# Shifting expert slots between stages of a fused attention and PEER kernel by its table of rates

## The chip, the cores and the metric

The kernel runs on one core of a Trainium2 chip, in one launch. The metric is the device time of that launch in microseconds (us). The core has a matrix engine (PE, TensorE), a vector engine (DVE), an activation engine (ACT), a general engine (POOL, GpSimd), a queue engine that issues most transfers (SP), and 16 DMA engines.

## The reference

One input x of 2048 tokens by 512 is layer-normalised, and two branches of it are added to x: attention with 32 heads of 16 over one shared key and value head, and PEER, a mixture of 4096 single-neuron experts. Per token and head PEER scores 64 + 64 sub-keys, keeps the two best of each, keeps the two best of the four sums, and adds two experts, weighted.

```
xn = _layernorm(x, axis=-1)
return x + _A_ref(xn, A_wq, A_wk, A_wv, A_wo) + _B_ref(xn, B_w_q, B_k1, B_k2, B_u, B_v)
# _A_ref: scores = q k^T / 4 for 32 heads, p = softmax, o = p v, o @ wo
# _B_ref: i1, i2 = two best sub-keys of 64 on each side; cand = t1 + t2 (2 x 2)
#         top_e = two best of the four; g = softmax of their scores
#         act = gelu(xn . u[top_e]);  out = sum g * act * v[top_e]
```

So a token has 64 experts (32 heads by 2), each a row of u (512) and a row of v (512).

## The kernel before, in words

Tokens lie in 16 tiles of 128 and in four phases of four tiles. All four phases need attention and sub-key scores. The experts are done in two ways. For phases 0 and 1 they are **sparse**: one slot is one expert choice of each of 128 tokens, 512 slots in all (2 phases, 8 chunks of heads, 4 tiles, 8 choices). For phases 2 and 3 they are **dense**: a matrix of gates over all 4096 experts is made from one-hot rows, and all experts are multiplied.

A slot goes through three steps, each a function of the kernel:

- `gather` (L1058): POOL issues an indirect DMA that fetches 128 rows of 1024 values, u and v of an expert side by side, 512 KB, into one of 12 buffers named g.
- `dot` (L1070): DVE multiplies the u half with xn and sums it (one custom instruction and one that reads the accumulator). After every fourth slot three small DVE instructions (L1079 to L1081), a Tanh on ACT (L1086) and one more on DVE (L1093) make the weights of four slots.
- `add` (L1105): DVE adds weight times the v half into the token tile's sum xa. Only then is the buffer free: `gather` of slot m waits for `add` of slot m - 12.

The order of every engine's instructions is written out by the program. After a prologue (norm, projections, first scores) the main loop has 256 steps, counted by d. In a step PE makes four score tiles of attention (`scores`, L379), ACT takes their Exp (L386, four per step), PE multiplies four tiles with the values (`pv`, L396), and between them stand other threads of work: the sub-key thread (`wp_make`: expert weights for the sub-key scores are made from w_q, L550 to L560; `item`: psc products L598, then max and index on DVE, L611 and L613), the one-hot rows of a dense phase (`onehot`, L859 to L862, and their products L892), and its dense products (L800, L938).

How many slots a step does is set by one number, `pos`, which grows each step by a rate that depends on the stage, `dense_on[0]`:

```
            if dense_on[0] == 1:
                pos += 2.6 if d < half * 3 // 4 else max(0.0, NSL - pos) / max(half - 3 - d, 1)
            else:
                pos += (2.5 if len(IDX) < NC * TPH else 2.3 if 0 <= d - since < 12 else 1.75, 0, 1.0, 1.5, 0.5)[dense_on[0]]

            todo = max(min(int(pos + 0.001), g_next[0]) - d_next[0], 0) if d else 0
```

Stage 0 is the sparse part of the loop (its first rate holds while the indices of phase 0, NC * TPH = 32 of them, aren't all chosen, which is where expert weights are made), 4 comes just ahead of a one-hot stage, 2 is the one-hot stage (there are two, one for each dense phase), 3 its end, 1 the dense products. `half` is 256. `g_next`, `d_next` and `a_next` count the slots gathered, dotted and added. So the dots of a step are capped by what has been gathered, and gathering goes on to `a_next` + 12 at most, at the end of a step. A step on DVE runs: max and index of the sub-key thread, its `todo` dots, then up to max(`todo`, 3) adds with the small instructions between them, then the gathers on POOL. In steps 22 and 23 no adds are made (`quiet`, set where a pair of attention units is finished). While `lent` is 2, two of the 12 buffers serve another tile.

Of the kernel before, what the change touches and what calls it, by code (L numbers as in the profile page):

```python
# [33 lines left out]
NC = 8  # L34
TPH = GT
# [20 lines left out]
def tile_kernel(ctx, tc, x, wq, wkv, wo, wqT, kT, uv, ub, vb, out):  # L56
# [450 lines left out]
    def experts_out(t):  # L507
        acc, last = ACC[t], t // GT == QB[3]
        assert last or t in DONE_A
        store(lambda: nc.sync.dma_start(d_part[t] if last else out[t * P:(t + 1) * P, :], acc))  # L510
        LIVE.discard(t)
# [106 lines left out]
    IDX, G = {}, {}  # L618
# [470 lines left out]
    def weigh(n):  # L1089
        if n not in WT and n < a_ready[0] // SB:  # L1090
            ga, th = GA.pop(n), TH.pop(n)
            w = small.tile([P, SB], F32, name="w", bufs=3)
            nc.vector.scalar_tensor_tensor(w, th, 1.0, ga, op0=OP.add, op1=OP.mult)  # L1093
            WT[n] = w
# [17 lines left out]
    def gathers(most):  # L1112
        while g_next[0] < NSL and g_next[0] < a_next[0] + NGB - lent[0] and most > 0:
            gather(g_next[0])
            g_next[0] += 1
            most -= 1

    def dots(to):
        while d_next[0] < min(to, NSL):
            dot(d_next[0])  # L1120
            d_next[0] += 1

    def adds(most):
        while a_next[0] < a_ready[0] and most > 0:
            add(a_next[0])
            a_next[0] += 1
            most -= 1

    def tanhs(to):
        while a_ready[0] + SB <= to:  # L1130
            tanh(a_ready[0] // SB)
            a_ready[0] += SB
# [7 lines left out]
    def run(fns):  # L1140
        todo = fns[:]
        fns.clear()
        for fn in todo:
            fn()
# [6 lines left out]
    def flush():  # L1151
        posts()
        for _ in range(2):
            for fns in (ON_ACT, LAST, LATER, BEHIND):
                run(fns)
            ON_ACT.extend(LATER_ACT)
            LATER_ACT.clear()
        run(ON_ACT)
        run(BEHIND)
# [36 lines left out]
    dense_on, quiet = [0], [0]  # L1196
# [3 lines left out]
    def run_scores(until=None, key=None):  # L1200
        while (until is not None and spent[0] < until) or (key is not None and key not in IDX):
            posts()
            try:
                cost = next(sgen)
            except StopIteration:
                spent[0] = 1e9
                posts()
                return
            if cost is None:

                if key is None:
                    return
                continue
            spent[0] += cost
# [70 lines left out]
    def score_steps(n):  # L1285
        for _ in range(n):
            spent[0] += next(sgen)
# [113 lines left out]
    with tc.manual_schedule(engines=ENGINES):  # L1401
        nc.vector.tensor_copy(PK["mm"][96:128], PK["mm"][:32])
        run(AFTER)
        score_steps(3)
        done0 = spent[0] - 5.4
        half = STEPS // 2
        pos, since = 0.0, half
        for d in range(half + 24):


            if dense_on[0] != 0:
                since = d
            if dense_on[0] == 1:
                pos += 2.6 if d < half * 3 // 4 else max(0.0, NSL - pos) / max(half - 3 - d, 1)
            else:
                pos += (2.5 if len(IDX) < NC * TPH else 2.3 if 0 <= d - since < 12 else 1.75, 0, 1.0, 1.5, 0.5)[dense_on[0]]

            todo = max(min(int(pos + 0.001), g_next[0]) - d_next[0], 0) if d else 0

            def mid():  # L1420
                post = POST[:]
                POST.clear()
                for act, _ in post:
                    act()
                tanhs(d_next[0])
                run(ON_ACT)
                ON_ACT.extend(LATER_ACT)
                LATER_ACT.clear()
                run(LAST)
                LAST.extend(LATER)  # L1430
                LATER.clear()
                rest = BEHIND[:]
                BEHIND.clear()

                dots(d_next[0] + todo - 1)
                if a_ready[0] > a_next[0]:
                    weigh(a_next[0] // SB)
                dots(d_next[0] + 1 if todo > 0 else 0)
                for _, fn in post:
                    fn()  # L1440
                sums = min(a_ready[0] - a_next[0], max(todo, 3) if d < half else 4)
                if dense_on[0] > 2:
                    sums = min(sums, 2)
                if quiet[0] > 0:
                    quiet[0] -= 1
                    sums = 0
                if dense_on[0] == 2:
                    run(CHAIN)

                def go():  # L1450
                    n = sums
                    while rest or CHAIN or n > 0:
                        if n > 0:
                            adds(1)
                            n -= 1
                        elif not rest:
                            run(CHAIN)
                        if CHAIN:
                            CHAIN.pop(0)()
                        if rest:  # L1460
                            rest.pop(0)()
                    gathers(4)

                    for _ in range(1 if d < half - 4 else NT):
                        if OUTS:
                            experts_out(OUTS.pop(0))

                if dense_on[0] == 2:
                    POST_FILL.append(go)
                else:  # L1470
                    go()

            aim = done0 + (FILL - done0) * (d + 1) / half if d < half else 1e6

            def fill():
                run_scores(until=min(aim, spent[0] + MOST))
                run(POST_FILL)

            att_steps(d, mid, fill)
        flush()  # L1480
        run(STORES)
        while a_next[0] < NSL:
            dots(NSL)
            run(CHAIN)
            tanhs(d_next[0])
            adds(SB)
            run(STORES)
            gathers(NGB)
        assert not OUTS
        run(STORES)  # L1490


def build(nc, tc, args):
    tile_kernel(tc, *args)
# [33 lines left out]
```

## Time and profile before

| | before |
|---|---|
| median of 3 runs | 1872.38 us (1865.34 to 1872.58) |
| the profiled execution | 1873.29 us |
| its span, first to last instruction | 1871.5 us |
| granted TensorE clock | 0.997 |
| DMA traffic | 489.72 MB, mean 262 GB/s |

The profiled execution is 1.79 us longer than its span. In the views below a row has the start and the length in us or the busy time and the number of instructions; L12 is line 12 of the kernel. A name such as g<-in_uv_dram,idx is tile written <- tiles read.

### The profile page before, as it was taken

The numbers are of one execution on the slowest core, as the hardware profiler recorded it, in microseconds if no ns is written. First come the engines' busy times: TensorE is split into PE (matmuls) and PEld (weight loads), VectorE is DVE, ScalarE is ACT, GpSimd is POOL, SyncE is SP. The second block draws the span as 40 slices with busy tenths as digits, with TensorE's granted clock in tenths as the row PEclk, the third lists the DMA queues.
The fourth block names the chain that finished last, engine by engine and source line by source line (L and its number), as shares of the span: only waits on it lengthen the run. The fifth ranks groups of instructions, "written<-read, shape, count | busy, mean of one in ns | idle before, by whom it ended". The sixth has DMA issues, their size and how long they took to land.

```text
span 1871.5 us, 34947 instructions
## 1 busy us (share of the span) xinstructions
PE 1809.2 (97%) x10989; PEld 954.7 (51%) x10989; DVE 1629.8 (87%) x6378; ACT 1287.6 (69%) x1745; POOL 690.4 (37%) x920
## 2 busy tenths in 40 slices
PE   7999998999999899999999999999998999999998
PEld 4644444555554345555555554555543455555553
DVE  6749988999898977999899897999979778999994
ACT  4357665555558987888777555556579877778874
POOL 1124533435442122444344453345522124444430
PEclk9999999999999999999999999999999999999999
DMA  9699896996764777988899996877636868998982
GB/s 322 216 301 399 302 324 211 368 328 234 241 197 131 250 236 226 279 266 287 268 296 320 337 316 227 281 239 249 236 97 220 255 192 285 286 304 281 282 278 100
DMA packets 243704, 489.72 MB, mean 262 GB/s; under 512 B 93748, under 2 KB 106420, under 8 KB 243516
## 3 DMA queue, kind: packets, MB, share of 16 engines
q0 software_dynamic: 73728, 268.47, 42.9%
q1 hardware_dynamic: 168572, 218.21, 35.9%
q8 instruction: 87, 1.43, 0.3%
q10 hardware_dynamic: 1216, 0.79, 0.1%
q14 instruction: 101, 0.83, 0.1%
HBM read 426.49 MB, written 55.61 MB: 258 GB/s over the span
## 4 chain that ended last, share of the span: by engine, by line
PE 73%; DVE 7%; DMA 6%; ACT 5%; issue 3%; SPq 0%; POOL 0%; ACTq 0%; DVEq 0%; POOLq 0%
PE pv L396 21%; PE psc L598 17%; PE sc L379 15%; PE pact L800 8%; PE pout L938 8%; ACT pt L386 3%; PE pwo L494 2%; DMA g<-in_uv_dram,idx 2%; DVE xa L1105 1%; DMA wk<-dw 1%; DVE g L1070 1%; DVE oh L859 1%; PE pw L550 1%; DMA rsb<-dinv 1%; DMA gy<-dg 1%
## 5 line engine op out<-in xcount | busy, mean ns | idle before, releaser
L386 ACT ACTIVATE pt<-sc 128x1024 f32<-128x1024 f32 x1024 | 994.7, 1028 | 439.6 <-PE sc L379 380.4
L1058 POOL DMA_INDIRECT g<-in_uv_dram,idx x512 | 553.5, 1081 | 944.5 <-DVE xa L1105 429.0
L396 PE MATMUL pv<-pt,vaug 128*32 128x512 f32 x4096 | 495.8, 602 | 0.0
L379 PE MATMUL sc<-qa,kaug 64*128 64x512 f32 x2048 | 389.8, 451 | 23.0 <-ACT pt L386 18.9
L598 PE MATMUL psc<-wk,xt 128*128 128x512 f32 x1536 | 389.9, 401 | 5.2 <-DVE wk L560 4.1
L1105 DVE SCALAR_TENSOR_TENSOR xa<-g,w,xa 128x512 f32<-128x512 f32 x512 | 372.3, 745 | 0.1
L1070 DVE CUSTOM_DVE_ANT_0 g<-g,xa 128x512 f32<-128x512 f32 x512 | 335.5, 682 | 18.5 <-DMA g<-in_uv_dram,idx 18.5
L598 PEld LDWEIGHTS psc<-wk,xt 128*128 128x128 f32 x1536 | 277.4, 188 | 110.1 <-issue 43.1
L379 PEld LDWEIGHTS sc<-qa,kaug 64*128 64x128 f32 x2048 | 157.5, 184 | 342.3 <-ACT pt L386 210.1
L396 PEld LDWEIGHTS pv<-pt,vaug 128*32 128x32 f32 x4096 | 107.2, 109 | 243.7 <-issue 243.7
L613 DVE FIND_INDEX8 i<-m,psc 128x8 uint32<-128x64 f32 x1024 | 206.6, 222 | 0.8 <-issue 0.8
L938 PE MATMUL pout<-wk,wd 128*128 128x512 f32 x768 | 195.3, 401 | 4.3 <-DVE gy L981 2.1
L800 PE MATMUL pact<-xt,wk 128*128 128x512 f32 x768 | 196.1, 400 | 0.0
L938 PEld LDWEIGHTS pout<-wk,wd 128*128 128x128 f32 x768 | 140.4, 187 | 52.5 <-issue 4.9
L800 PEld LDWEIGHTS pact<-xt,wk 128*128 128x128 f32 x768 | 139.3, 188 | 48.8 <-issue 18.6
L611 DVE MAX8 m<-psc 128x8 f32<-128x64 f32 x1024 | 146.3, 215 | 18.2 <-PE psc L598 15.3
L765 DVE TENSOR_TENSOR wk<-rw,wk 128x512 fp32r<-128x512 f32 x128 | 85.2, 684 | 9.5 <-ACT wk L764 9.5
L941 DVE TENSOR_TENSOR da<-da,pout 128x512 f32<-128x512 f32 x128 | 83.1, 681 | 5.3 <-PE pout L938 5.0
L859 DVE TENSOR_TENSOR oh<-oh 128x2048 f16<-128x2048 f16 x64 | 78.0, 1219 | 2.7 <-ACT oh L826 2.7
L764 ACT CAST wk<-rw 128x512 fp32r<-128x512 f32 x128 | 74.1, 634 | 0.0
L613 DVE MATCH_VALUE_LOAD i<-m,psc 128x8 f32 x1024 | 72.4, 71 | 0.5 <-DVE i L613 0.5
L1093 DVE SCALAR_TENSOR_TENSOR w<-gth,ga 128x4 f32<-128x4 f32 x128 | 20.2, 158 | 50.7 <-ACT gth L1086 47.5
(162 smaller groups left out, 1315.2 us busy)
## 6 DMA issues: line engine op xcount, KB each, us to landing
wk<-dw SPq DMA_DIRECT2D x96, 512.0 KB
wqt<-in_wqT_dram SPq DMA_DIRECT2D x32, 512.0 KB
dw<-wk SPq DMA_DIRECT2D x32, 512.0 KB
rw<-in_ub_dram SPq DMA_DIRECT2D x64, 256.0 KB
rw<-in_vb_dram SPq DMA_DIRECT2D x64, 256.0 KB
gy<-dg SPq DMA_DIRECT2D x64, 256.0 KB
dg<-gst SPq DMA_DIRECT2D x14, 928.0 KB
g<-in_uv_dram,idx POOLq DMA_INDIRECT x512
```

The lines of the kernel that those rows point to most:

```text
L379: nc.tensor.matmul(p[:, b, :], kaug[o:o + 64, kc * P:(kc + 1) * P], QA[u][o:o + 64, i, :], start=True, stop=True)
L386: nc.scalar.activation(PT[u, kc, i], p, AF.Exp, scale=SCALE)
L396: nc.tensor.matmul(PV[u][32 * j:32 * j + 32, :], vaug[:, kc, :], pt[:, b, :], start=kc == 0, stop=kc == 15)
L598: nc.tensor.matmul(p, XT[k][:, a, j * P:(j + 1) * P], WC[n_][k][:, bb, :], start=n == 0, stop=n == 11)
L611: nc.vector.max(m8[:, jb, s, :], p[:, s * E:(s + 1) * E])
L613: nc.vector.max_index(i8[:, jb, s, :], m8[:, jb, s, :], p[:, s * E:(s + 1) * E])
L800: nc.tensor.matmul(p, us[:, a, k * P:(k + 1) * P], XT[k][:, c, :], start=n == 0, stop=n == 11)
L859: nc.vector.tensor_tensor(out=oa, in0=num(P), in1=bc(0, tb, P), op=OP.is_equal)
L938: nc.tensor.matmul(p, wd[0][:, a, j * P:(j + 1) * P], vs[:, c, :], start=n == 0, stop=n == 5)
L1058: nc.gpsimd.indirect_dma_start(out=gt, out_offset=None, in_=uv, in_offset=bass.IndirectOffsetOnAxis(ap=IDX[ph, c, ti][:, s:s + 1], axis=0))
L1070: nc.vector.tensor_tensor_reduce(u, u, XN[TPH * ph + ti], scale=1.0, scalar=0.0, op0=OP.mult, op1=OP.add, accum_out=a[:, i:i + 1])
L1105: nc.vector.scalar_tensor_tensor(acc, v, w[:, i:i + 1], acc, op0=OP.mult, op1=OP.add)
```

## The change

Two rates in the table change. While phase 0's indices are being chosen, a step does 2.8 slots instead of 2.5. In the one-hot stage of the first dense phase (d below 128), it does 0.5 instead of 1.0; the one-hot stage of the second dense phase keeps 1.0.

```
-                pos += (2.5 if len(IDX) < NC * TPH else 2.3 if 0 <= d - since < 12 else 1.75, 0, 1.0, 1.5, 0.5)[dense_on[0]]
+                pos += (2.8 if len(IDX) < NC * TPH else 2.3 if 0 <= d - since < 12 else 1.75, 0, 0.5 if d < half // 2 else 1.0, 1.5, 0.5)[dense_on[0]]
```

The order of the instructions on PE is the same in both kernels; on DVE, ACT and POOL the slots' instructions stand at other places, and a few transfers on SP with them. No tile and no transfer is added or taken away. Following the counters through the loop, before has 80 slots dotted after step 31 and the change 89; after step 60 it is 130 and 140, and after step 80, near the end of the first one-hot stage, 150 and 151.

On DVE at step 28 and the start of step 29, before (ISA rows of L1070 are dots, L1105 are adds, L611 and L613 belong to the sub-key thread, the numbers are those of buffers). The dots are those of slots 70 and 71, the adds those of slots 62 to 64:

```order
L1070 ISA g_3852,act_3920<-g_3852,xa_159 128x512
L1070 ISA act_3920 128x1
L1070 ISA g_3931,act_3920<-g_3931,xa_161 128x512
L1070 ISA act_3920 128x1
L1105 SCALAR_TENSOR_TENSOR xa_163<-g_3636,w_3923,xa_163 128x512
L1079 SCALAR_TENSOR_TENSOR gq_4016<-act_3920 128x4
L1093 SCALAR_TENSOR_TENSOR w_4021<-gth_4012,ga_3919 128x4
L1105 SCALAR_TENSOR_TENSOR xa_165<-g_3638,w_3923,xa_165 128x512
L1080 SCALAR_TENSOR_TENSOR gy_4017<-gq_4016,act_3920 128x4
L1105 SCALAR_TENSOR_TENSOR xa_159<-g_3640,w_4021,xa_159 128x512
```

The same place with the change, step 27, where the dots are those of slots 74 to 76 and the adds those of slots 65 to 67:

```order
L1070 ISA g_3893,act_3879<-g_3893,xa_159 128x512
L1070 ISA act_3879 128x1
L1070 ISA g_3895,act_3879<-g_3895,xa_161 128x512
L1070 ISA act_3879 128x1
L1070 ISA g_3897,act_3968<-g_3897,xa_159 128x512
L1070 ISA act_3968 128x1
L1105 SCALAR_TENSOR_TENSOR xa_161<-g_3445,w_3887,xa_161 128x512
L1079 SCALAR_TENSOR_TENSOR gq_3965<-act_3879 128x4
L1105 SCALAR_TENSOR_TENSOR xa_159<-g_3447,w_3887,xa_159 128x512
L1080 SCALAR_TENSOR_TENSOR gy_3966<-gq_3965,act_3879 128x4
L1093 SCALAR_TENSOR_TENSOR w_3974<-gth_3961,ga_3878 128x4
L1105 SCALAR_TENSOR_TENSOR xa_161<-g_3449,w_3887,xa_161 128x512
```

Before, the next step's first dot (slot 72) uses a buffer that add 60 freed a step earlier, and only its third (slot 74) uses one that add 62, above, frees. With the change the next step's three dots (77, 78, 79) use the three buffers that the adds above (65, 66, 67) free.

On DVE in the first one-hot stage, before: the one-hot rows (L859, L861, L862) with the dots of slots 144 and 145 and the adds of slots 140 to 142 between them:

```order
L1070 ISA g_7813,act_8403<-g_7813,xa_163 128x512
L1070 ISA act_8403 128x1
L859 TENSOR_TENSOR oh_8415<-oh_7451,oh_7453 128x2048
L861 TENSOR_TENSOR oh_7537<-oh_7451,oh_7453 128x512
L862 TENSOR_TENSOR oh_7537<-oh_7537,oh_7453 128x512
L1105 SCALAR_TENSOR_TENSOR xa_159<-g_7326,w_8401,xa_159 128x512
L1105 SCALAR_TENSOR_TENSOR xa_161<-g_7328,w_8401,xa_161 128x512
L1105 SCALAR_TENSOR_TENSOR xa_159<-g_7809,w_8401,xa_159 128x512
L1070 ISA g_7893,act_8403<-g_7893,xa_165 128x512
L1070 ISA act_8403 128x1
```

The same stage with the change, from the dot of slot 146 on:

```order
L1070 ISA g_7103,act_7813<-g_7103,xa_163 128x512
L1070 ISA act_7813 128x1
L859 TENSOR_TENSOR oh_8112<-oh_7511,oh_7513 128x2048
L861 TENSOR_TENSOR oh_7596<-oh_7511,oh_7513 128x512
L862 TENSOR_TENSOR oh_7596<-oh_7596,oh_7513 128x512
L859 TENSOR_TENSOR oh_8135<-oh_7511,oh_7513 128x2048
L861 TENSOR_TENSOR oh_7596<-oh_7511,oh_7513 128x512
L862 TENSOR_TENSOR oh_7596<-oh_7596,oh_7513 128x512
L859 TENSOR_TENSOR oh_8189<-oh_7511,oh_7513 128x2048
L861 TENSOR_TENSOR oh_7596<-oh_7511,oh_7513 128x512
L862 TENSOR_TENSOR oh_7596<-oh_7596,oh_7513 128x512
```

There is now a dot in every second step of this stage instead of in every step, and its adds come half as often. From step 32 to step 60 both kernels do 1.75 slots per step, the change some ten slots further on.

## The prediction

> **What bounds the kernel now.** First the page: which engine is busy and which one the chain of waits runs over.
>
> ```profile
> PE 1809.2 (97%) x10989; PEld 954.7 (51%) x10989; DVE 1629.8 (87%) x6378; ACT 1287.6 (69%) x1745; POOL 690.4 (37%) x920
> PE 73%; DVE 7%; DMA 6%; ACT 5%; issue 3%; SPq 0%; POOL 0%; ACTq 0%; DVEq 0%; POOLq 0%
> ```
>
> PE is busy nearly throughout and carries most of the chain. Its work is not touched, so the time can only change where PE waits: 62.3 us in all (1871.5 - 1809.2). Where that is shows the view of busy time by stage. I cut it at starts of steps, found by counting the Exp instructions (L386), four per step: the first row is steps 0 to 23 (expert weights are made), the second steps 24 to 31 (their end, up to where phase 0's indices are complete), the third steps 32 to 64, the fourth steps 65 to 80 (first one-hot stage); the last is a piece of the second.
>
> ```profile
> core 0: us, PE busy (x) PEld busy (x) DVE busy (x) ACT busy (x) POOL busy (x), PEclk, DMA share, GB/s
> 102.30:287.40 185.10, 178.32 (x1008) 84.70 (x1008) 150.89 (x757) 122.11 (x166) 73.09 (x93) 1.00 0.91 320
> 287.40:349.70 62.30, 58.52 (x329) 28.92 (x327) 54.93 (x282) 36.92 (x50) 29.71 (x41) 0.97 0.82 291
> 349.70:580.60 230.90, 229.15 (x1314) 126.82 (x1316) 211.84 (x1356) 137.62 (x171) 106.76 (x207) 1.00 0.76 253
> 580.60:663.20 82.60, 72.28 (x864) 33.35 (x856) 81.04 (x158) 77.64 (x105) 12.97 (x11) 1.00 0.57 184
> 320.00:325.00 5.00, 5.00 (x26) 1.33 (x25) 5.00 (x26) 2.48 (x4) 1.49 (x2) 0.66 0.95 324
> ```
>
> In the third row PE is the bound: 33 steps in 230.9 us, 7.0 us each, PE busy 99%. In the fourth, DVE is busy 81.04 of 82.6 us and ACT 77.64, so DVE is the bound and ACT stands close behind it. The second row is odd: 7.79 us a step (62.3 / 8), with PE and DVE both idle at times. What holds it, the chain of waits in that stretch tells:
>
> ```profile
> 292.43 5.69 DMA g<-in_uv_dram,idx
> 298.14 0.69 DVE g L1070
> 298.84 0.66 DVE xa L1105
> ...
> 301.44 5.29 DMA g<-in_uv_dram,idx
> 306.76 0.69 DVE g L1070
> ...
> 309.64 5.61 DMA g<-in_uv_dram,idx
> 315.27 0.69 DVE g L1070
> ```
>
> This is a ring: an add frees a buffer, a gather of 512 KB fills it in 5.29 to 5.69 us, a dot reads it, and the adds that free the next buffers stand behind that dot on DVE. It arises as no adds are made in steps 22 and 23 while dots go on: the 12 buffers run out, and three slots remain between what is dotted and what is gathered. Before leaves the ring by itself, since at 2.5 slots every second step has two dots and three adds.
>
> **The change part by part.** The price of a slot on DVE comes from the groups view:
>
> ```profile
> L1105 DVE SCALAR_TENSOR_TENSOR xa<-g,w,xa 128x512 f32<-128x512 f32 x512 | 372.3, 745 | 0.1
> L1070 DVE CUSTOM_DVE_ANT_0 g<-g,xa 128x512 f32<-128x512 f32 x512 | 335.5, 682 | 18.5 <-DMA g<-in_uv_dram,idx 18.5
> L1070 DVE DVE_READ_ACCUMULATOR2_ANT act<- 128x1 f32 x512 | 41.6, 81 | 0.0
> L1093 DVE SCALAR_TENSOR_TENSOR w<-gth,ga 128x4 f32<-128x4 f32 x128 | 20.2, 158 | 50.7 <-ACT gth L1086 47.5 <-issue 3.0
> L1080 DVE SCALAR_TENSOR_TENSOR gy<-gq,act 128x4 f32<-128x4 f32 x128 | 20.2, 158 | 1.2
> L1079 DVE SCALAR_TENSOR_TENSOR gq<-act 128x4 f32<-128x4 f32 x128 | 20.2, 158 | 0.4
> L1081 DVE TENSOR_TENSOR ga<-act,gg 128x4 f32<-128x4 f32 x128 | 20.1, 157 | 0.0
> ```
>
> A slot costs 0.682 + 0.081 + 0.745 and a quarter of the four small ones (0.631 / 4 = 0.158): 1.67 us of DVE. The Tanh on ACT, one per four slots, and the gather on POOL (busy 48% at most in these rows) move along and bind nothing.
>
> *Steps 1 to 24.* 62 dots become 68 and 53 adds 59: 6 slots, 10.0 us more for DVE. DVE idles 34.2 us there (185.1 - 150.89), so on average it fits: 161 of 185 us. But PE already idles 6.8 us at this load, and a DVE with less room answers psc and wk later. Between 0 (all in idle time) and +10.0 (all on the path) I take **+2.0**, close to the end that the idle time supports.
>
> *Steps 25 to 32, the ring.* Here the change bites. Following the counters: in before, slots whose buffer was freed only in the step ahead are three in step 25, two in 26, two in 27, and one in 28 and 29. With 2.8 slots nearly every step asks for three dots, and adds are three as well, so the distance between dotted and gathered stays at three: all three dots of each of steps 25 to 31, and both of step 32, wait for gathers issued at the end of the step before. How long a turn of the ring is shows POOL in order of time (a gather's issue):
>
> ```profile
> 292.43 0.94 POOL L1058 DMA_INDIRECT g<-in_uv_dram,idx  x1 [0.31 <-DVE m L611]
> ...
> 301.44 0.94 POOL L1058 DMA_INDIRECT g<-in_uv_dram,idx  x1 [0.30 <-DVE m L611]
> 302.68 0.94 POOL L1058 DMA_INDIRECT g<-in_uv_dram,idx  x1 [0.31 <-issue]
> ...
> 309.64 1.20 POOL L1058 DMA_INDIRECT g<-in_uv_dram,idx  x1 [0.31 <-DVE xa L1105]
> ```
>
> The third gather of step 24 starts at 292.43 and its dot was waited for; the third of step 25 starts at 302.68. A turn with three fresh dots is 10.25 us. With two fresh dots it runs from second gather to second gather: 301.44 to 309.64, 8.20 us. So the change takes 7 turns of 10.25 and one of 8.20 from step 24 to step 32: 79.95 us. Before needs, from the first add of step 24 to that of step 32:
>
> ```profile
> 288.59 0.75 DVE L1105 SCALAR_TENSOR_TENSOR xa<-g,w,xa 128x512 f32<-128x512 f32 x1
> ...
> 355.83 0.75 DVE L1105 SCALAR_TENSOR_TENSOR xa<-g,w,xa 128x512 f32<-128x512 f32 x1
> ```
>
> 67.24 us, in which DVE has fallen 5 us further behind PE (1.2 us after the step's start at 287.4, 6.1 after that at 349.7); I allow the change the same lag and no more, since PE already waits for DVE's wk in this stretch. Difference: **+12.7 us**. Ends: if all turns were 8.20 us, 65.6 - 67.24 = -1.6. If a gather took as long as the slowest that the chain shows,
>
> ```profile
> 122.88 10.12 DMA g<-in_uv_dram,idx
> ```
>
> a turn would be 4.4 us longer, and eight of them +48; that was one gather, in a stage with a DMA share of 0.91 and right at the loop's start, while the ring's own three lie within 0.4 us of each other, at a share of 0.82. I stay with these. The Trainium skill (DMA: Bandwidth & Descriptors, Anatomy of one DMA) prices a GpSimd transfer at about 2.0 us plus its bytes over 436e3 per us, 3.2 us for 512 KB as an estimate; by it a turn would be about 7.8 us and this term would vanish. The rows above don't agree with it here: 5.29 to 5.69.
>
> *Steps 33 to 64.* The lead of ten slots stays, the rate is 1.75 in both: nothing.
>
> *Steps 65 to 80.* 16 dots and 16 adds become 8 and 8: 8 x 1.67 = 13.3 us less for DVE, 67.7 us busy. ACT's 77.64 us then bind, so of 82.6 us at most 5.0 can go; the least is 0. I take **-3.5**, nearer the upper end, as ACT's Exp still wait at times for score tiles that PE makes behind the one-hot products.
>
> *After step 81* the change is one slot ahead until it evens out: nothing.
>
> Sum against the profiled execution: 1873.29 + 2.0 + 12.7 - 3.5 = 1884.5, so **1884 us**. The median before is 0.9 us lower; the same shift from it gives 1883.6.
>
> **The rivals.**
>
> *The gathers keep up (not slower).* The ring's turn falls to what PE needs, because a slower ring also thins the traffic that its gathers share. It decides where a gather lands in about 2.3 us (10.25 - 7.0 = 3.25 less than 5.6) or where PE, which needs psc and wk from DVE, can run ahead through the stretch. Then steps 24 to 32 cost no more than before, or lose their old waits, and what is left is the one-hot gain: 1873.3 - 5.0 = 1868 to 1873.3 + 2.0 - 3.5 = 1872. For it: DVE has room on average, in every row. Against it: the three gathers of the ring took 5.69, 5.29 and 5.61 us and grew no faster as the ring slowed. By the skill's formula above this rival would win.
>
> *Stalls cool PE (slower still).* PE in order of time, before and behind the one long wait of this stretch:
>
> ```profile
> 310.46 1.92 PE L396 MATMUL pv<-pt,vaug 128*32 128x512 f32 x16
> ...
> 318.91 0.96 PE L598 MATMUL psc<-wk,xt 128*128 128x512 f32 x3 [2.72 <-DVE wk L560]
> ...
> 320.53 3.49 PE L396 MATMUL pv<-pt,vaug 128*32 128x512 f32 x16
> ```
>
> After 2.72 us idle the same 16 products take 3.49 us in place of 1.92, and the granted clock is 0.66 (row 320 to 325 above). If each of seven turns paid that 1.57 us on the path: 11.0 us more, 1895. I hold it for mostly hidden, since PE has 3.25 us to spare in a turn. The Trainium skill (TensorE: Matmul & The Clock Gate, Part 1) has the clock halve after an idle window of about 3.4 us; the trace agrees on the slowdown, here after a shorter wait. Gathers that land later in busier traffic lead to the same region.
>
> *DVE fills up ahead of the ring.* The 10 us of steps 1 to 24 land on the path: 1892.
>
> *The rate isn't followed.* The cap on gathers could undo the higher rate; but the counters show 89 slots for 80 after step 31, so the ring slows the steps and does not thin them: 1873.
>
> **How the numbers follow.** Forecast 0.55 (by its own terms 1878 to 1893: ring +10 to +15, steps 1 to 24 0 to +5, one-hot -5 to 0), gathers keep up 0.22, PE cools or gathers slow 0.15, DVE full 0.05, rate not followed 0.03. The range cuts about a tenth on either side: 1869 to 1900. A measurement of this kernel can tell about 0.5% from no change, 9.4 us: faster means below 1863.9, which only a full one-hot gain and a vanished ring could near: 0.03. Slower is above 1882.7: the upper two thirds of the forecast (0.37) and the two rivals above it (0.20), 0.57. The rest is the same, 0.40.
>
> **What would show it.** Right: the waits of DVE's dots for gathers grow from 5.4 us in this stretch,
>
> ```profile
> DVE g L1070 <- DMA g<-in_uv_dram,idx: 5.4, 5, 1.6
> ```
>
> to some 20 us (a turn of 10.25 less 6.9 us of DVE work, 54.93 / 8, seven times), nearly all between the ends of steps 24 and 32; these eight steps take 72 to 78 us in place of 62.3; the chain there shows seven or eight gathers; and the 16 one-hot steps take 78 to 80 us, with DVE below 70 us busy. Wrong: if the eight steps stay near 62 us, the ring is no bound and the first rival holds; if the one-hot steps don't get shorter, DVE was not what held them; if steps 1 to 23 grow by more than 5 us, DVE's room was an average only.

## The result, and the profile after

| | before | after |
|---|---|---|
| median | 1872.48 us (6 runs, 1865.34 to 1878.13) | 1893.81 us (6 runs, 1890.16 to 1902.01) |
| ratio to before | | 1.0129 [1.0108, 1.0151] |
| the profiled execution | 1873.29 us | 1902.01 us |
| its span | 1871.5 us | 1900.2 us |

The change makes the kernel 1.3% slower. The profiled execution of it was the slowest of its six; the experiments below ran the same kernel once more, and that profile (1892.69 us, span 1890.9) lies near the median. Both are used here and called the first and the second profile.

The page of the first: busy time per engine, and the shares of the chain of waits.

```profile
PE 1816.9 (96%) x10989; PEld 958.8 (50%) x10989; DVE 1629.4 (86%) x6378; ACT 1288.5 (68%) x1745; POOL 688.0 (36%) x920
PE 74%; DVE 9%; DMA 6%; ACT 3%; issue 1%; SPq 0%; DVEq 0%; ACTq 0%
```

DVE, ACT and POOL do what they did. PE's 10989 instructions are the same and take 7.7 us more, and PE's idle time has grown from 62.3 to 83.3 us (1900.2 - 1816.9). Where, shows the view of busy time by stage, cut at the same steps as before; here the first profile for steps 0 to 23, 24 to 31, 32 to 64 and 65 to 80, then 24 to 32 together.

```profile
core 0: us, PE busy (x) PEld busy (x) DVE busy (x) ACT busy (x) POOL busy (x), PEclk, DMA share, GB/s
101.70:292.50 190.80, 180.00 (x1008) 85.23 (x1008) 158.93 (x781) 122.59 (x167) 78.73 (x99) 0.99 0.92 326
292.50:364.20 71.70, 61.41 (x327) 29.91 (x325) 51.00 (x258) 36.86 (x50) 26.66 (x39) 0.93 0.74 248
364.20:608.10 243.90, 232.22 (x1314) 127.78 (x1318) 218.40 (x1390) 137.55 (x172) 112.45 (x211) 0.97 0.73 245
608.10:688.80 80.70, 71.37 (x864) 33.01 (x856) 74.32 (x133) 77.43 (x103) 7.89 (x6) 1.00 0.48 161
292.50:383.60 91.10, 69.83 (x368) 34.32 (x366) 61.97 (x332) 41.41 (x55) 30.58 (x42) 0.89 0.76 254
```

Steps 24 to 31 grew by 9.4 us (71.7 against 62.3), and the 33 steps behind them by 13.0. Nearly all of the latter is step 32: 383.6 - 364.2 = 19.4 us, against 6.8 before. PE, which had run ahead of DVE, waits for it there. So the region has to be cut behind step 32, and there before reads

```profile
287.40:356.50 69.10, 65.32 (x368) 32.67 (x366) 61.59 (x335) 41.40 (x56) 33.10 (x46) 0.98 0.84 295
```

69.1 us against 91.1. The view of waits of the first profile in these nine steps says who waits: engine, line, for what, us in total, times, longest.

```profile
DVE g L1070 <- DMA g<-in_uv_dram,idx: 28.1, 17, 5.7
PE psc L598 <- DVE i L613: 10.8, 1, 10.8
PE psc L598 <- DVE wk L560: 7.4, 2, 5.4
```

The dots wait 28.1 us for gathers, 17 times, and PE waits behind them, most of it once, at the end. The chain of waits of the second profile (start, us, what) gives seven gathers, one at the start of each of seven turns:

```profile
296.64 5.95 DMA g<-in_uv_dram,idx
...
307.14 5.24 DMA g<-in_uv_dram,idx
...
317.04 5.34 DMA g<-in_uv_dram,idx
...
326.86 7.43 DMA g<-in_uv_dram,idx
...
338.77 6.51 DMA g<-in_uv_dram,idx
...
349.85 6.58 DMA g<-in_uv_dram,idx
...
361.08 10.16 DMA g<-in_uv_dram,idx
```

A turn runs from one of these starts to the next: 10.50, 9.90, 9.82, 11.91, 11.08, 11.23, and the last runs to the gather at 375.73, shown further below, 14.65. The ring is there in every step from 24 to 31. Three turns are as long as forecast, four are longer, and their gathers landed later.

Lengths of stages in us, from the profiles of both kernels and of the experiments below (steps found as in the prediction):

| steps | before | after, 1st | after, 2nd | same_after_81 | no_ring | keep_three | middle_instead | rate_265 |
|---|---|---|---|---|---|---|---|---|
| 0 to 7 | 67.0 | 69.4 | 70.7 | 69.0 | 71.5 | 71.5 | 67.1 | 67.8 |
| 8 to 23 | 118.1 | 121.4 | 120.3 | 120.3 | 121.3 | 119.2 | 118.0 | 118.3 |
| 24 to 32 | 69.1 | 91.1 | 87.3 | 89.3 | 65.4 | 65.5 | 69.7 | 83.5 |
| 65 to 80 | 82.6 | 80.7 | 80.6 | 80.4 | 80.4 | 80.4 | 80.3 | 80.3 |

### The profile page after: what moved, and what is told of

Its sections match the earlier page's. It is cut to its first block, busy times and chain, and to the rows that moved or that the text cites. A ratio compares the mean times of both kernels' runs of the same rounds, so it can differ in the third digit from the quotient of the medians.

```text
span 1900.2 us, 34942 instructions
## 1 busy us (share of the span) xinstructions
PE 1816.9 (96%) x10989; PEld 958.8 (50%) x10989; DVE 1629.4 (86%) x6378; ACT 1288.5 (68%) x1745; POOL 688.0 (36%) x920
## 4 chain that ended last, share of the span: by engine, by line
PE 74%; DVE 9%; DMA 6%; ACT 3%; issue 1%; SPq 0%; DVEq 0%; ACTq 0%
PE pv L396 21%; PE psc L598 16%; PE sc L379 15%; PE pact L800 9%; PE pout L938 9%; DMA g<-in_uv_dram,idx 3%; PE pwo L494 2%; DVE xa L1105 2%; ACT pt L386 2%; DVE g L1070 1%; DMA gy<-dg 1%; DVE oh L859 1%; DMA rw<-in_vb_dram 1%; DVE m L611 1%; PE pw L550 1%
## 5 line engine op out<-in xcount | busy, mean ns | idle before, releaser
L1058 POOL DMA_INDIRECT g<-in_uv_dram,idx x512 | 551.4, 1077 | 977.7 <-DVE xa L1105 380.0
L1105 DVE SCALAR_TENSOR_TENSOR xa<-g,w,xa 128x512 f32<-128x512 f32 x512 | 374.2, 746 | 0.0
L1070 DVE CUSTOM_DVE_ANT_0 g<-g,xa 128x512 f32<-128x512 f32 x512 | 336.3, 684 | 44.1 <-DMA g<-in_uv_dram,idx 42.7
L613 DVE FIND_INDEX8 i<-m,psc 128x8 uint32<-128x64 f32 x1024 | 206.8, 224 | 0.0
L611 DVE MAX8 m<-psc 128x8 f32<-128x64 f32 x1024 | 146.5, 216 | 28.1 <-PE psc L598 27.5
L859 DVE TENSOR_TENSOR oh<-oh 128x2048 f16<-128x2048 f16 x64 | 78.0, 1219 | 4.1 <-ACT oh L826 2.6
L613 DVE MATCH_VALUE_LOAD i<-m,psc 128x8 f32 x1024 | 74.9, 73 | 0.0
L657 POOL CAST fi<-i 128x64 f32<-128x64 uint32 x32 | 8.9, 280 | 137.8 <-DVE i L613 137.6
```

The lines of the kernel that those rows point to most:

```text
L611: nc.vector.max(m8[:, jb, s, :], p[:, s * E:(s + 1) * E])
L613: nc.vector.max_index(i8[:, jb, s, :], m8[:, jb, s, :], p[:, s * E:(s + 1) * E])
L859: nc.vector.tensor_tensor(out=oa, in0=num(P), in1=bc(0, tb, P), op=OP.is_equal)
L1058: nc.gpsimd.indirect_dma_start(out=gt, out_offset=None, in_=uv, in_offset=bass.IndirectOffsetOnAxis(ap=IDX[ph, c, ti][:, s:s + 1], axis=0))
L1070: nc.vector.tensor_tensor_reduce(u, u, XN[TPH * ph + ti], scale=1.0, scalar=0.0, op0=OP.mult, op1=OP.add, accum_out=a[:, i:i + 1])
L1105: nc.vector.scalar_tensor_tensor(acc, v, w[:, i:i + 1], acc, op0=OP.mult, op1=OP.add)
```

## The experiments

**The change once more** gives a second profile. Here and below, the ratio is to the kernel before as it ran beside the kernel in question.

> The changed kernel itself once more, with a fresh profile. Its first profile was 28.7 us longer in span than before: 5.7 in steps 0 to 23, 22.0 in steps 24 to 32 (the ring of gathers), 7.9 in step 126 (one wait of DVE for the gates gy), and some 7 less in other places. Theory A (all three places are made by the order of instructions and come in every execution): 1890 to 1900 us, step 126 is again 12 us or longer. Theory B (step 126 was a single disturbed transfer): step 126 is about 6.9 us and the time nearer 1886.

Measured: 1895.27 us, ratio 1.0121 [1.0083, 1.0159]. In the first profile a single step far behind the change, step 126, had taken 14.7 us against 6.9 before: DVE waited 7.7 us for a load of dense gates.

```profile
996.92 11.80 DMA gy<-dg
```

In the second profile, with the order of instructions unchanged, the step is short again (last row of the stages of the second profile):

```profile
292.20:379.40 87.20, 69.04 (x368) 34.33 (x366) 61.91 (x332) 41.44 (x55) 30.23 (x42) 0.90 0.78 261
604.10:684.70 80.60, 71.29 (x864) 33.06 (x856) 74.28 (x133) 77.36 (x103) 7.90 (x6) 1.00 0.50 161
998.00:1005.60 7.60, 6.99 (x41) 3.75 (x39) 5.05 (x13) 5.95 (x10) 1.13 (x2) 1.00 1.03 348
```

So those 7.8 us belong to one execution and not to the change.

**Nothing moved behind step 81.** After step 80 the change is one slot ahead. A slightly lower one-hot rate takes that away.

```
-... 0.5 if d < half // 2 else 1.0 ...
+... 0.5 - 1.1 / 17 if d < half // 2 else 1.0 ...
```

> The change, but with a first one-hot rate of 0.5 - 1.1/17, so that from step 81 on the slots are the same as before (151 dotted, not 152) and SP's loads of phase 1's tiles stand again behind the loads of rw and gy. The ring is untouched. Theory A (one slot of lead moves those loads ahead of rw and gy on SP, which then wait for a store): step 126 is 6.9 us, about 8 us less than the changed kernel, 1884 to 1887. Theory B (disturbance, or DVE's load): no difference from the changed kernel, about 1893.

Measured: 1895.31 us, 1.0115 [1.0080, 1.0150], the same as the change beside it. What the change costs lies ahead of step 81. The next kernels build on this one where said.

**No pause in steps 22 and 23** (on same_after_81). The ring needs the pause, which runs the buffers down.

```
-                if d < 28:
+                if d < 20:
                     quiet[0] = 2
```

> As same_after_81, and adds go on in steps 22 and 23 (the pause after the pair of units at step 21 is left out), so that no dot of steps 25 to 33 needs a gather of the step just ahead; the same slots are dotted per step but for two. Theory A (the ring is the cost): steps 24 to 32 take about 9 x 7.0 = 63 us, less than before's 69.1; with 5 us for steps 0 to 23 and 3.5 gained in the one-hot stage 1866 to 1872. Rival (DVE is simply too full at 2.8 slots a step, and the ring only shows it): steps 24 to 32 stay above 75 us, 1880 or more.

Measured: 1870.98 us, 0.9983 [0.9967, 0.9999], and steps 24 to 32 in 65.5 us:

```profile
294.80:360.30 65.50, 63.80 (x368) 32.51 (x366) 61.40 (x339) 41.43 (x56) 30.75 (x44) 1.00 0.91 310
```

DVE is as busy as in the change (61.40 and 61.91 us) in 22 us less, and PE's clock is 1.00. So in these nine steps the rate of 2.8 and DVE's load are harmless, and the ring is the whole cost. Steps 0 to 23 still take 192.8 us against 185.1 before, so the higher rate isn't free there; in the total, the shorter steps 24 to 32 and the one-hot stage make up for most of it.

**Three gathered slots always in hand** (on same_after_81): another way out of the ring. The pause stays, but in steps 21 to 47 a step's dots stop three short of what has been gathered.

```
-            todo = max(min(int(pos + 0.001), g_next[0]) - d_next[0], 0) if d else 0
+            todo = max(min(int(pos + 0.001), g_next[0] - (3 if 20 < d < 48 else 0)) - d_next[0], 0) if d else 0
```

> As same_after_81 with the pause of adds in steps 22 and 23 kept, but in steps 21 to 47 dots stop three slots short of what has been gathered, so that none waits for a gather of the step just ahead; the slots held back are made up by step 48. Theory A: the ring is broken as in no_ring by another means, steps 24 to 32 take 63 to 68 us and the time is within 4 us of no_ring, 1867 to 1875. Rival (the pause itself is the cost, in that DVE loses two steps of adds and has to catch up): steps 24 to 32 stay above 75 us, 1880 or more.

Measured: 1865.24 us, 0.9961 [0.9943, 0.9979], which by the ratios is 1.5% or about 29 us under same_after_81, and the stage:

```profile
293.10:358.50 65.40, 63.70 (x368) 32.52 (x366) 61.33 (x335) 41.27 (x54) 33.52 (x45) 1.00 0.90 311
```

Two different edits that only break the ring give the same 65.4 to 65.5 us, and both are below before's 69.1: before, whose dots wait 5.4 us there, pays part of the ring too. The stage gives 23.9 of the 29 us (89.3 - 65.4); where the rest comes from was not taken apart.

**Half the step in the rate**, 2.65 where before has 2.5 and the change 2.8, with the one-hot rate set so that nothing moves behind step 81.

```
-... (2.5 if len(IDX) < NC * TPH else ... 1.0, 1.5, 0.5) ...
+... (2.65 if len(IDX) < NC * TPH else ... 1.0 - 4.80 / 17 if d < half // 2 else 1.0, 1.5, 0.5) ...
```

> Half the change: 2.65 slots a step early instead of 2.8, and the first one-hot rate lowered by just as many slots (4.8), so that from step 81 on all is as before. By the counters every step from 25 to 30 still asks for three slots gathered in the step ahead. Theory A (the ring sets the time): six turns of three fresh dots at 10.3 to 12 us and one of two, so steps 24 to 32 take 82 to 86 us, nearly all of the change's 87 to 91, and the time is 1886 to 1890. Rival (cost in proportion to the slots that are added early): half of the change's extra, 78 to 80 us there, 1882 or less.

Measured: 1881.59 us, 1.0055 [1.0036, 1.0074]; the stage:

```profile
288.60:372.10 83.50, 70.41 (x368) 34.61 (x366) 61.29 (x330) 41.51 (x55) 30.35 (x42) 0.90 0.79 265
```

Half the step in the rate costs 83.5 - 69.1 = 14.4 us in this stage, of the second profile's 18.1: four fifths of the cost for half of the slots, so it does not grow in proportion to them. The total is below the 1886 to 1890 us that were expected. Steps 0 to 23 cost only 0.9 us here; and the steps behind 126, in which the two kernels do the same, took 880.5 us in this profile against 886.0 before, which no edit explains.

**Before without the pause**: is there something to be won in before?

```
-                if d < 28:
+                if d < 20:
                     quiet[0] = 2
```

> The kernel before with the pause of adds in steps 22 and 23 left out, nothing else. Before has the ring too, for four steps. Theory A: steps 24 to 32 go from 69.1 to 64 to 66 us, 1868 to 1871. Rival (the pause keeps the reciprocal of the softmax sums and its transfers on time, and without it they cost what the ring saves): no change, 1872 to 1876.

Measured: 1870.85 us, 1.0002 [0.9983, 1.0021]. The dots' waits for gathers are gone, but steps 23 and 24 take 10.1 and 11.4 us in place of 8.4 and 8.0. The view of waits, 280 to 360 us:

```profile
DVE w L1093 <- ACT gth L1086: 4.8, 2, 3.0
...
PE pwt L557 <- DVE i L613: 2.5, 1, 2.5
```

DVE now waits for a Tanh of ACT ahead of an add, the adds that the pause held back stand ahead of its answers to PE, and PE waits for these. That this makes up the whole loss is a reading of the order, not shown by a run: in no_ring, also without the pause, the same two steps take 9.3 and 8.0 us. What is shown is that in before, leaving the pause out saves about as much as it costs. Keeping slots in hand leaves the pause and avoids the ring.

**The slots moved elsewhere**: early rate as before, the nine slots into steps 33 to 60.

```
-... 2.3 if 0 <= d - since < 12 else 1.75, 0, 1.0, 1.5, 0.5) ...
+... 2.3 if 0 <= d - since < 12 else 1.75 + 8.5 / 29 if d < 61 else 1.75, 0, 0.5 if d < half // 2 else 1.0, 1.5, 0.5) ...
```

> The one-hot half of the change alone, with the early rate left at 2.5: 0.5 slots a step in the first one-hot stage, and the 8.5 slots moved to steps 32 to 60 (1.75 + 8.5/29 a step), where there is no ring. From step 81 on as before. Theory A: steps 65 to 80 get 2 to 5 us shorter, nothing else moves, 1867 to 1870. Rival (steps 32 to 60 have no room: DVE 92% busy there becomes 98%): they get longer by 3 us or more and the time is 1872 or above.

Measured: 1870.6 us, 0.9974 [0.9956, 0.9992]. The steps that take the slots don't get longer (223.9 us for steps 33 to 64, 224.1 before), and the one-hot steps give 2.3 us (82.6 to 80.3).

**What makes the last landings late.** The view of SP in order of time (a row joins issues of one line) of the second profile, in the stretch of the late landings, and behind it POOL's last gather of the ring:

```profile
326.01 3.58 SPq L566 DMA_DIRECT2D dw<-wk  x2
329.69 4.01 SPq L572 DMA_DIRECT2D wk<-dw  x2
337.84 4.42 SPq L566 DMA_DIRECT2D dw<-wk  x2
342.35 1.50 SPq L572 DMA_DIRECT2D wk<-dw  x2
343.95 17.34 SPq L1172 DMA_DIRECT2D xt<-dxt  x16
361.34 2.66 SPq L572 DMA_DIRECT2D wk<-dw  x4
...
375.73 0.94 POOL L1058 DMA_INDIRECT g<-in_uv_dram,idx  x1 [0.31 <-DVE i L613]
```

From 326 us on SP issues stores of expert weights, reads of them and the next phase's token tiles; the seven gathers' late four start at 326.86 and after. How much all queues moved while a gather landed shows the view of busy time, its last number in GB/s; three of the seven:

```profile
317.04:322.38 5.34, 4.00 (x25) 2.80 (x21) 2.89 (x20) 3.23 (x6) 0.94 (x1) 1.00 0.71 241
349.85:356.43 6.58, 6.58 (x41) 3.52 (x39) 2.27 (x13) 3.88 (x4) 0.94 (x1) 1.00 1.06 355
361.08:371.24 10.16, 6.05 (x36) 3.07 (x34) 3.00 (x20) 2.75 (x4) 0.94 (x1) 1.00 0.98 342
```

That is 1.3, 2.3 and 3.5 MB (length times GB/s), and the three gathers of a step are 1.6 MB: in these three the landing grows with what is moved beside it. Two kernels on same_after_81 take transfers away. The first leaves the xt loads out:

```
-        if more and nph != ph:
+        if more and nph != ph and n_ != NC - 1:
             load_xt(nph, j)
```

> As same_after_81, but the 16 transfers of phase 1's transposed rows (xt<-dxt, 2 MB, issued by SP in the ring's last turns) are left out, so phase 1's scores come from phase 0's rows. The ring's last turn took 14.7 to 15.9 us, its gather landed in 10.2 to 11.4. Theory A (the gathers of the last turns land late as they share the DMA queues with SP's transfers): the last turn falls to 10.3 to 12 us, steps 24 to 32 to 84 to 86 us. Rival (the last turn is long for what PE and DVE do in it): it stays at 14 us or more, and steps 24 to 32 near 88.

Measured: 1891.11 us in one run, steps 24 to 32 in 86.1 us. The landing ahead of the last, which had stood beside the xt loads, is short now, and its turn is 9.86 us in place of 11.23; the last is still late:

```profile
351.49 5.20 DMA g<-in_uv_dram,idx
361.35 10.30 DMA g<-in_uv_dram,idx
```

SP's next four reads had moved up to stand beside it. The row joins them, issued from 358.40 on, with two that were issued at 343.52 and 344.00:

```profile
343.52 17.32 SPq L572 DMA_DIRECT2D wk<-dw  x6
```

The second leaves out four of SP's reads as well (chunk n = NC uses the tiles that are there):

```
         for k in ks:
+            if n == NC:
+                WC.setdefault(n, []).append(WC[n - 1][k])
+                continue
             wk = wk_tile()
```

> As no_xt_load, and the four reads of stored weights (wk<-dw, 2 MB) for the next chunk, which there simply took the place of the xt loads, are left out too: that chunk's scores use the chunk before's weights. In the ring's last three turns SP then moves nothing large. Theory A (gathers land late where SP's transfers share the queues): the third gathers of steps 29 to 31 land in 5 to 6 us in place of 6.5 to 10.3, these turns take 10 to 10.7 us, steps 24 to 32 81 to 84 us. Rival (the last turns are long for another reason): a landing of 10 us again in the last turn, 86 us or more.

Measured: 1885.44 us in one run, the stage in 82.6 us, and in the chain

```profile
326.65 7.26 DMA g<-in_uv_dram,idx
...
338.40 6.78 DMA g<-in_uv_dram,idx
...
349.74 6.32 DMA g<-in_uv_dram,idx
...
360.71 5.23 DMA g<-in_uv_dram,idx
```

The last landing falls from 10.30 to 5.23 us, and POOL's next third gather starts at 370.42 (three lines were added to this kernel, so its L1061 is L1058 of the others):

```profile
370.42 0.94 POOL L1061 DMA_INDIRECT g<-in_uv_dram,idx  x1 [0.31 <-DVE i L616]
```

That turn is 9.71 us (370.42 - 360.71) in place of 14.65. So SP's reads beside the gather made it late. The three turns before it stayed at 11.8, 11.3 and 11.0 us with landings of 7.26 to 6.32: SP's stores at 326 to 342 us were still there, and the four reads that are left stood at 342 to 345, behind the stores. With no_xt_load, the cause is shown for the last two of the four late landings. For the first two no kernel took the stores and reads beside them away; the traffic fits (in the second profile 2.5 and 2.4 MB were moved while they landed), but there it is not shown.

**A slow start** (on same_after_81): 2.5 slots in steps 0 to 3, then a little more than 2.8. In the second profile the third dot of step 2 had waited for a gather that was issued at the loop's start:

```profile
131.60 0.69 DVE L1070 CUSTOM_DVE_ANT_0 g<-g,xa 128x512 f32<-128x512 f32 x1 [8.76 <-DMA g<-in_uv_dram,idx]
```

```
-... (2.8 if len(IDX) < NC * TPH else ...
+... (2.5 if d < 4 else 2.8 + 1.2 / 28 if len(IDX) < NC * TPH else ...
```

> As same_after_81, but the first four steps keep the rate of 2.5 and the rest has 2.84, so that the lead at step 32 is the same. Theory A on steps 0 to 23 (the third dot of step 2 needs a gather that is issued only at the loop's start and lands behind SP's loads; that wait, and the clock after it, is half of the loss there): steps 0 to 7 go from 69 to 71.5 back to 67 to 67.5 us, steps 8 to 23 stay 1 to 3 us longer than before, the ring is as long as before this edit. Rival (DVE's load over all 24 steps makes it): steps 0 to 7 stay at 69 or above.

Measured: 1892.78 us in one run. Steps 0 to 7 take 66.6 us in place of 69.0 to 70.7, as expected; steps 8 to 15 take 61.8, 3.0 more than the kernel it was built on, so nothing was won.

**Put together**, for a kernel better than both. The first is middle_instead with three slots in hand (the two edits above); the second also spreads the slots of the second one-hot stage over the steps ahead of it.

> A version meant to beat both: middle_instead (2.5 early, the one-hot stage's 8.5 slots moved to steps 32 to 60) with dots that stop three slots short of the gathers in steps 21 to 47. Theory A: steps 0 to 23 as before (185), steps 24 to 32 65 to 66 us (before 69.1), the one-hot stage 2 us shorter: 6 us less than before, 1864 to 1868 where before is 1871 to 1874. Rival (what the ring no longer costs is lost elsewhere, as in before_no_pause): no different from middle_instead, ratio 0.997 to 1.000.

Measured: 1861.65 us, 0.9952 [0.9937, 0.9966].

```
-... 1.75 + 8.5 / 29 if d < 61 else 1.75, 0, 0.5 if d < half // 2 else 1.0, 1.5, 0.5) ...
+... 1.75 + 8.5 / 29 if d < 61 else 1.75 + 8.5 / 34, 0, 0.5, 1.5, 0.5) ...
```

> As middle_keep_three, and the second one-hot stage has the rate 0.5 too, its 8.5 slots moved to the steps from 146 to 179. Theory A: that stage (steps 184 to 199, 85.3 us before) gets 2 us shorter as the first did: 1862 to 1866 where before is 1871 to 1874. Rival (the steps from 146 on, or the dense stage after it, have no room for them): no gain over middle_keep_three.

Measured: 1858.52 us, 0.9940 [0.9916, 0.9963], the fastest of all. Its steps 24 to 32, and its first one-hot stage:

```profile
287.40:352.60 65.20, 63.72 (x368) 32.50 (x366) 61.27 (x337) 41.41 (x55) 33.22 (x45) 1.00 0.89 307
575.20:654.90 79.70, 71.51 (x864) 32.87 (x856) 73.18 (x131) 77.21 (x103) 7.76 (x6) 1.00 0.50 166
```

Its lead over middle_keep_three is inside the two intervals. What the second one-hot stage gave is not resolved: it took 82.3 us against 84.0, and it varies from 81.8 to 86.7 among kernels that do not touch it.

## Why the prediction was right or wrong

The direction and the mechanism held: the slots were bought in the one stage where a ring of gather, dot and add sets the pace, and no_ring and keep_three show that the loss in that stage is the ring's. The size did not: 1884 forecast, 1893.81 measured, about twice the loss. The time lies inside the range of 1869 to 1900. Three terms came out higher than forecast, and the total would be 4 to 5 us further off but for the last row below, places where the change does no other work. That is luck: no run explains it, and the steps behind 126 alone took from 880.5 to 888.9 us among kernels that do the same there. Term by term, as differences of spans of the profiles:

| term | forecast | 1st profile | 2nd profile |
|---|---|---|---|
| steps 0 to 23 | +2.0 | +5.7 | +5.9 |
| steps 24 to 32, the ring | +12.7 | +22.0 | +18.1 |
| steps 33 to 64 | 0 | +0.4 | +0.6 |
| steps 65 to 80 | -3.5 | -1.9 | -2.0 |
| step 126 | 0 | +7.8 | +0.7 |
| the rest | 0 | -5.3 | -3.9 |
| span | +11.2 | +28.7 | +19.4 |

*The ring*, forecast at +12.7 us and measured at +22.0 and +18.1, is the term that failed most, at the sentence "I stay with these": three landings of 5.29 to 5.69 us were taken for all turns, and the last four took 6.51 to 10.16. The turn of 10.25 us was right where it was measured: the first three turns of the second profile sum to 30.22 us against 30.75. The last four sum to 48.87 against 41.0, 7.9 more; their landings sum to 30.68 us against four times the mean of the three sampled ones, 22.1, which is 8.6 more. So the excess of the turns is the landings'. (All seven turns are 7.3 us over the forecast, more than the 5.4 by which the stage missed it; the 2 us between them were not taken apart.) The three sampled gathers landed between 298 and 315 us, and the trace of before had, in SP's order of time, what comes behind them:

```profile
318.88 3.58 SPq L566 DMA_DIRECT2D dw<-wk  x2
322.56 3.36 SPq L572 DMA_DIRECT2D wk<-dw  x2
...
333.72 21.18 SPq L1172 DMA_DIRECT2D xt<-dxt  x16
```

I took the price of a turn from the quiet half of the stretch and laid it over the busy half. The busy half had its price in the trace of before as well: taking the packets of POOL's queue in order, 144 to a gather, the last packet of the third gather of a step came 5.0 to 5.2 us after its issue up to 315 us, and 6.8 to 10.7 us after it from 318 to 356. The bound was there (a gather of 10.12 us), and was dismissed as one of another stage; the last landing came to 10.16 and 11.41. The formula of the Trainium skill (DMA: Bandwidth & Descriptors, Anatomy of one DMA), an estimate of 3.2 us for 512 KB, is further off still, though it prices one transfer and these gathers are the third of three issued within some 3 us: of the gathers that set a turn in the two profiles of the change, none landed in under 5.24 us, and in the kernel with the fewest transfers beside it none in under 5.23.

*Steps 0 to 23* were set "close to the end that the idle time supports", +2.0, and came to +5.7 and +5.9, past the 5 us that the prediction named as the sign that DVE's room was an average only. One part is seen: a dot of step 2 now waits 8.76 us at the loop's start, and slow_start took 2.4 to 4.1 us out of steps 0 to 7. It came back in steps 8 to 15, which fits DVE being full there, but that was not taken apart further.

*The one-hot steps* lost 2.0 us, where 3.5 was forecast. ACT is now busy 77.36 us of 80.6. DVE's busy time fell only to 74.3 and not to 67.7: the groups view of the stage counts 9 dots in place of 16 and 8 adds in place of 15, some 11 us less, but also 31 one-hot rows of each kind in place of 29 or 30, 3 us more. Which of them fall into the cut depends on how far DVE is behind PE, and 8 slots times 1.67 us left that out.

```profile
L859 DVE TENSOR_TENSOR oh<-oh 128x2048 f16<-128x2048 f16 x31 | 37.7, 1217 | 1.5 <-PE pg L892 1.5
L1070 DVE CUSTOM_DVE_ANT_0 g<-g,xa 128x512 f32<-128x512 f32 x9 | 6.2, 684 | 0.0
L1105 DVE SCALAR_TENSOR_TENSOR xa<-g,w,xa 128x512 f32<-128x512 f32 x8 | 5.8, 745 | 0.0
```

The row to L859 shows DVE waiting for PE's products now, 1.5 us in all. So DVE no longer sets the pace alone, and the upper end of 5.0 was no place to lean to.

*The expected sights.* The dots' waits came as 28.1 us for about 20. The eight steps 24 to 31 took 71.7 us in the first profile and 69.1 in the second, under the 72 to 78, because the end of the ring fell into step 32. The one-hot steps ended just above the 78 to 80 us.

*The rivals.* That the gathers keep up is refuted by the chain. That the rate is not followed, too. That DVE is full ahead of the ring had 10 us of steps 0 to 23 on the path; somewhat more than half of it came. Stalls do cool PE, as the rival had it; PE in order of time, second profile:

```profile
326.04 1.65 PE L598 MATMUL psc<-wk,xt 128*128 128x512 f32 x3 [5.01 <-DVE wk L560]
...
328.77 3.03 PE L396 MATMUL pv<-pt,vaug 128*32 128x512 f32 x16
...
376.96 1.65 PE L598 MATMUL psc<-wk,xt 128*128 128x512 f32 x3 [9.60 <-DVE i L613]
...
379.69 3.17 PE L396 MATMUL pv<-pt,vaug 128*32 128x512 f32 x16
```

Sixteen products take 3.03 and 3.17 us behind such waits in place of 1.92, and over the nine steps PE is busy 69.04 us for the same 368 instructions that took 65.32: 3.7 us in all, where the rival had put 11. How much of the 3.7 lies on the path no run separated. The late landings alone (8.6 us) are as large as the excess of the four turns (7.9). The rival's other clause, gathers that land later in busier traffic, is what happened.

## What to carry to other kernels

Work that runs through a ring of buffers is priced by the turn (transfer, use, release), not by the busy time of its engines: here the higher rate cost nothing in steps 24 to 32 as long as a few fetched buffers lay between what was asked for and what had been fetched, and once that distance was used up every step cost a full turn. Take a transfer's duration from the rows that stand beside the traffic it will meet, along the whole stretch, and not from the first few of it. Where a pause drains such a ring, keep a few fetched buffers in hand through it: that was worth more here (about 29 us against the change, and half a per cent below before with the slots moved to another stage) than the choice among the three rates tried.

## What the runs showed of the hardware

An indirect gather of 512 KB, the third of three issued within some 3 us, took from 5.24 to 11.41 us from issue to landing in the same nine steps of the two profiles. With SP's loads beside it gone, the last of them came down from 10.30 to 5.23 us: transfers that another engine issues can double a gather's time. Leaving out only one of the two groups of these loads did nothing for that gather, as the other moved up into its place; the gather ahead of it, which had stood beside the first group, landed after 5.20 us in place of 6.58.
